# A two-layer MLP on one core: another load schedule, one VectorE semaphore, and a finer split of the last output tile

## Chip, cores, metric

One core of one Trainium2 chip. The metric is the device time of one execution in microseconds (us), as a median of several executions; lower is better. "Span" is the part of an execution that the profile covers; here the time is the span plus about 2.1 us. "Granted clock" is the TensorE clock that the chip allowed, as a share of full speed. An execution counts as fast when it is no more than 1.5% above the fastest of its kernel; all comparisons use fast executions unless the text says otherwise.

## The reference

```python
# B, S, D, F = 1, 2048, 640, 1536, everything bf16
def reference(x, w1, b1, w2, b2):
    h = jnp.einsum("bsd,df->bsf", x, w1) + b1
    r = jnp.where(h > 0, h, 0)
    h = r * r
    return jnp.einsum("bsf,fd->bsd", h, w2) + b2
```

The kernel feeds its first product with x transposed, D on the partitions (`xT`).

## The kernel before

The 2048 tokens are cut into four chunks of 512. PE (the TensorE) works in this order: dummy matmuls, transposes of chunk 0 on PE, first product of chunk 0, first product of chunk 1, second product of chunk 0, first product of chunk 2, second product of chunk 1, and so on. A first-product group is 5 matmuls of 512 columns, a second-product group 12 matmuls of 320 columns. ScalarE applies the relu, VectorE squares, and VectorE also adds b2 and writes the output tile ("eviction").

x arrives in two ways. Chunks 0 and 1 are loaded as they are and transposed on PE with an identity matrix, into PSUM, from where VectorE copies them to `xT`. Chunks 2 and 3 are transposed by the DMA engines. The transposes of chunk 1 stand between groups of chunk 0's first product:

```python
for ft in range(FT):
    G1(ft, 0, CH)
    while tc1 and tc1[0] == ft:            # t_c1_after = (7, 8, 9, 10)
        tc1.pop(0)
        items.append(("T", ...))           # one token tile of chunk 1: 5 PE transposes
...
# sync engine: plain loads first, and only when all have landed the DMA transposes
xn_load(0); xn_load(1)
for i in range(len(w1pieces)): w1_load(i)
for h in range(2, NXH): xn_load(h)         # chunk 1, plain
# ... waits for every load of x, b1, w1, b2, w2 ...
for i, (r0, n) in enumerate(xpieces):      # chunks 2 and 3
    sp.dma_start_transpose(out=xT[:, :, r0:r0 + n], in_=x2[r0:r0 + n, :]).then_inc(sx[i], 16)
for (t, c0, ncols, need) in stores:
    sp.wait_ge(s_o, need)
    sp.dma_start(out=..., in_=o_sb[:, t, c0:c0 + ncols]).then_inc(s_out, 16)
# ... b2 and w2 are loaded by GpSimd once w1 has landed
```

VectorE runs the same item list in order: for `("T", st)` it copies a transposed tile from PSUM, for a first-product group it squares, for a second-product group it evicts. Each kind has its own semaphore (`s_cb`, `s_c`, `s_sq`, `s_o`). The last output tile is two groups of 320 columns, each stored by itself.

## Time and profile before

| | before |
|---|---|
| time, median | 117.18 us (116.68 to 117.58, 4 runs) |
| span of the profiled execution | 114.604 us |
| PE busy | 110.3 us (96%) |
| first matmul of the first product starts | 6.35 us |
| last matmul ends | 112.07 us |

The head of the page of before: span, then busy time of each engine with its share of the span.

```profile
span 114.6 us, 1595 instructions
PE 110.3 (96%) x683; PEld 65.6 (57%) x683; DVE 39.8 (35%) x91; ACT 34.5 (30%) x50; POOL 4.0 (4%) x10
```

PE is the limit. Where PE loses time is told by the chain of waits of before: start, duration, engine and line, number of instructions. L289 are dummies, L310 PE transposes, L237 the copy to `xT`, L342 the first product, L368 the second, L256 the eviction.

```profile
1.12 3.17 PE ps L289 x15
4.29 0.29 PE ps L310 x5
4.61 1.70 DVE xT L237 x4
6.35 8.81 PE ps L342 x40
15.16 0.28 PE ps L310 x5
15.44 1.08 PE ps L342 x5
...
19.27 0.70 ACT r_sb L215
19.97 0.02 issue
19.99 0.42 DVE h2T L244
20.42 0.41 DVE xT L237
20.83 0.05 issue
20.88 13.12 PE ps L342 x60
34.00 13.04 PE ps L368 x96
47.04 12.95 PE ps L342 x60
...
85.98 26.09 PE ps L368 x192
112.07 0.02 issue
112.10 0.49 DVE o_sb L256
```

Read it as a budget. An undisturbed chunk of 60 first-product matmuls takes 12.95 us (216 ns each), 96 second-product matmuls 13.04 us (136 ns each). Between 15.16 and 20.88 us two things stand in the way: PE spends 0.28 us on each of four token tiles of chunk 1, and then the chain leaves PE. Chunk 1 cannot start before the last of its copies, which stands on VectorE behind a square, which waits for a relu. From 6.35 to 34.00 us two chunks of first product take 27.65 us; at 216 ns a matmul the 120 would take 25.9.

Four DMA transposes ran alone in before. The view of stretches (stretch, its length, busy time and count of each engine, PE clock, DMA share, GB/s) shows the DMA engines full at half the rate of plain loads (175 GB/s at a DMA share of 1.00, beside 358 at 1.09; over the neighbouring stretches 175 to 179, beside 327 to 358):

```profile
8.50:10.50 2.00, 2.00 (x11) 0.92 (x10) 0.78 (x2) 1.37 (x2) 0.00 (x0) 1.00 1.09 358
24.50:26.50 2.00, 2.00 (x12) 0.88 (x10) 0.80 (x2) 1.22 (x3) 0.00 (x0) 1.00 1.00 175
```

The last store in the timeline of before is issued 0.03 us after the last eviction ends (112.10 + 0.49 = 112.59):

```profile
112.62 0.33 SPq L202 DMA_DIRECT2D out_dram<-o_sb  x1
```

### The profile page before, as it was taken

Reading aid. Unit: us, or ns where it says so; the run is one execution under the profiler, and the core shown is the slowest. Engines: PE = TensorE matmul, PEld = TensorE weight load, DVE = VectorE, ACT = ScalarE, POOL = GpSimd, SP = SyncE. Lnnn points to the kernel's source line nnn. Section 1 sums busy time; section 2 is a strip of 40 time slices with the busy share of each in tenths; the row PEclk is TensorE's granted clock in tenths of the full one; section 3 lists DMA queues with packets and bytes.
Section 4 is the critical chain, followed back from the end, with each engine's and each line's share of the span. In section 5 each row is a group of like instructions: output and inputs, shape, how many; then the busy total and the mean of one; then the engine's idle time right before and its main releaser. Section 6 shows DMA issues by size and latency. Waiting matters only on the chain.

```text
span 114.6 us, 1595 instructions
## 1 busy us (share of the span) xinstructions
PE 110.3 (96%) x683; PEld 65.6 (57%) x683; DVE 39.8 (35%) x91; ACT 34.5 (30%) x50; POOL 4.0 (4%) x10
## 2 busy tenths in 40 slices
PE   6989999999999999999999999999999999999991
PEld 4834455344447777544447777544447777777770
DVE  1323445444343333243343332243433332333231
ACT  5026564465761000156651000157562000000000
POOL 4000900000000000000000000000000000000000
PEclk9999999999999999999999999999999999999999
DMA  2999499069900111000000111010000110111111
GB/s 62 348 342 371 89 301 350 30 132 166 160 0 6 57 57 57 33 27 0 0 6 0 57 57 54 10 51 6 0 0 0 57 57 31 32 57 57 57 57 57
DMA packets 11414, 9.43 MB, mean 82 GB/s; under 512 B 5744, under 2 KB 10480, under 8 KB 11408
## 3 DMA queue, kind: packets, MB, share of 16 engines
q1 hardware_dynamic: 10896, 7.21, 22.3%
q0 software_dynamic: 512, 2.13, 5.8%
q8 instruction: 5, 0.08, 0.3%
q14 instruction: 1, 0.01, 0.0%
HBM read 5.41 MB, written 2.62 MB: 70 GB/s over the span
## 4 chain that ended last, share of the span: by engine, by line
PE 94%; DVE 3%; ACT 1%; issue 0%
PE ps L368 46%; PE ps L342 45%; PE ps L289 3%; DVE xT L237 2%; PE ps L310 1%; ACT r_sb L215 1%; DVE o_sb L256 0%; DVE h2T L244 0%; DVE scr L225 0%
## 5 line engine op out<-in xcount | busy, mean ns | idle before, releaser
L342 PE MATMUL ps<-xT,w1s 128*128 128x512 bf16 x240 | 53.1, 379 | 0.6 <-DVE xT L237 0.6
L368 PE MATMUL ps<-w2s,h2T 128*128 128x320 bf16 x384 | 52.6, 299 | 0.0
L215 ACT ACTIVATE r_sb<-ps,b1s 128x512 bf16<-128x512 f32 x48 | 33.0, 687 | 51.4 <-PE ps L342 51.4
L368 PEld LDWEIGHTS ps<-w2s,h2T 128*128 128x128 bf16 x384 | 37.6, 98 | 15.1
L342 PEld LDWEIGHTS ps<-xT,w1s 128*128 128x128 bf16 x240 | 23.1, 98 | 28.0 <-DVE xT L237 1.4
L244 DVE TENSOR_TENSOR h2T<-r_sb 128x512 bf16<-128x512 bf16 x48 | 20.4, 426 | 34.0 <-ACT r_sb L215 34.0
L256 DVE TENSOR_TENSOR o_sb<-ps,b2s 128x320 bf16<-128x320 f32 x32 | 15.7, 492 | 34.5 <-PE ps L368 34.5
L237 DVE COPY xT<-ps 128x640 bf16<-128x640 bf16 x8 | 3.6, 484 | 3.4 <-PE ps L310 3.4
L289 PE MATMUL ps<-scr 128*128 128x256 bf16 x18 | 3.7, 381 | 1.1 <-DVE scr L225 1.1
L289 PEld LDWEIGHTS ps<-scr 128*128 128x128 bf16 x18 | 2.3, 137 | 1.9 <-DVE scr L225 1.1
L310 PEld LDWEIGHTS ps<-ident,xn 128*128 128x128 bf16 x40 | 2.7, 98 | 1.0
L310 PE MATMUL ps<-ident,xn 128*128 128x128 bf16 x40 | 3.1, 219 | 0.0
L388 POOL DMA_DIRECT2D w2s<-in_w_dram x3 | 2.3, 763 | 0.0
L208 ACT ACT_TABLE_LOAD x1 | 1.3, 1283 | 0.8 <-PEq L402 0.8
L386 POOL DMA_DIRECT2D b2s<-in_b_dram x1 | 0.6, 615 | 8.9 <-DMA w1s<-in_w_dram 8.9
L379 POOL DMA_DIRECT2D b1row<-in_b_dram x1 | 0.7, 664 | 0.8 <-POOLq L402 0.8
L225 DVE MEMSET scr<- 128x128 f32 x1 | 0.2, 165 | 0.9 <-PEq L402 0.9
L381 POOL TENSOR_SCALAR_AFFINE_SELECT ident<-ones 128x128 bf16<-128x128 bf16 x1 | 0.3, 314 | 0.1
L208 ACT ACTIVATE scr<-scr 128x8 bf16<-128x8 bf16 x1 | 0.2, 208 | 0.0
L294 PE MATMUL ps<-ident,b1row 12*128 12x12 bf16 x1 | 0.2, 176 | 0.0
L226 DVE MEMSET ones<- 128x128 bf16 x1 | 0.2, 165 | 0.0
L232 DVE COPY b1s<-ps 128x12 bf16<-128x12 bf16 x1 | 0.2, 155 | 0.0
(5 smaller groups left out, 0.5 us busy)
## 6 DMA issues: line engine op xcount, KB each, us to landing
out_dram<-o_sb SPq DMA_DIRECT2D x15, 160.0 KB, 1.8
w2s<-in_w_dram POOLq DMA_DIRECT2D x3, 640.0 KB, 7.9
xn<-in_x_dram SPq DMA_DIRECT2D x4, 320.0 KB, 5.1
w1s<-in_w_dram SPq DMA_DIRECT2D x2, 640.0 KB, 6.7
w1s<-in_w_dram SPq DMA_DIRECT2D x2, 320.0 KB, 4.7
b2s<-in_b_dram POOLq DMA_DIRECT2D x1, 160.0 KB, 4.2
out_dram<-o_sb SPq DMA_DIRECT2D x2, 80.0 KB, 1.6
xT<-in_x_dram SPq DMA_TRANSPOSE x4, 4.7
```

Source lines behind the costliest of these rows:

```text
L208: act.activation(out=scr2[:], in_=scr[:, 0:8], func=ACT_FN.Relu)
L215: act.activation(out=r_sb[:, ft, c0:c0 + ncols], in_=ps[:, gi % 4, 0:ncols], func=ACT_FN.Relu, bias=b1s[:, ft:ft + 1], scale=1.0,).then_in ...
L237: v.tensor_copy(out=xT[:, :, st * P:(st + 1) * P], in_=psT(st)[:, 0:KT * P].rearrange("p (k c) -> p k c", k=KT),).then_inc(s_c, 1)
L244: v.tensor_tensor(out=h2T[:, ft, c0:c0 + ncols], in0=r_sb[:, ft, c0:c0 + ncols], in1=r_sb[:, ft, c0:c0 + ncols], op=AluOpType.mult,).then_ ...
L256: v.tensor_tensor(out=o_sb[:, t, c0:c0 + ncols], in0=ps[:, 4 + qi % 4, 0:ncols], in1=b2s[:, c0:c0 + ncols], op=AluOpType.add,).then_inc(s_ ...
L289: pe.matmul(ps[:, bank, 0:256], scr[:, 0:P], scr[:, 0:256], start=True, stop=True)
L310: mm = pe.transpose(out=psT(st)[:, k * P:(k + 1) * P], in_=xn[:, st, k * P:(k + 1) * P], identity=ident[:],)
L342: mm = pe.matmul(ps[:, gi % 4, 0:ncols], w1s[:, k, ft * P:(ft + 1) * P], xT[:, k, c0:c0 + ncols], start=(k == 0), stop=(k == KT - 1),)
L368: mm = pe.matmul(ps[:, 4 + qi % 4, 0:ncols], h2T[:, ft, t * P:(t + 1) * P], w2s[:, ft, c0:c0 + ncols], start=(ft == 0), stop=(ft == FT - 1),)
L379: g.dma_start(out=b1row[:], in_=b1.rearrange("(ft p) -> ft p", p=P)).then_inc(s_b1, 16)
L386: g.dma_start(out=b2s[:], in_=b2.partition_broadcast(P)).then_inc(s_b2, 16)
L388: g.dma_start(out=w2s[:, f0:f0 + n, :], in_=w2v[:, f0:f0 + n, :]).then_inc(sw2[i], 16)
```

## The change

Four edits with these intents: chunk 1 also comes by DMA transpose, queued right behind w1, so PE does not transpose it; b2 and w2 go to the same sync queue and no transfer waits for another any more; all VectorE results count on one semaphore and one-time waits are hoisted into the group before the one that needs them, to save waits at group heads; the last output tile is cut into 320, 192, 64 and 64 columns, so that the last eviction and store are short.

```diff
-    t_c1_after=(7, 8, 9, 10),
+    last_split=(320, 192, 64, 64),
...
-    NXN = 2 * STC
+    NXN = STC
-    xpieces = [(r0, XR) for r0 in range(2 * CH, S, XR)]
+    xpieces = [(r0, XR) for r0 in range(CH, S, XR)]
...
             if t == ST - 1:
+                c0 = 0
+                for n in cfg["last_split"]:
+                    G2(t, c0, n)
+                    c0 += n
...
-        while tc1 and tc1[0] == ft:
-            tc1.pop(0)
-            items.append(("T", STC + (len(cfg["t_c1_after"]) - len(tc1)) - 1))
... sync engine
+            for h in range(NXH):
+                xn_load(h)
             for i in range(len(w1pieces)):
                 w1_load(i)
-            (waits for all loads)
+            xT_load(1)
+            sp.dma_start(out=b2s[:], ...).then_inc(s_b2, 16)
+            for (f0, n) in w2pieces:
+                sp.dma_start(out=w2s[...], in_=w2v[...]).then_inc(s_w2, 16)
+            for c in range(2, NCH):
+                xT_load(c)
... VectorE: every .then_inc(s_cb | s_c | s_sq | s_o, 1) becomes
+            .then_inc(s_dve, 1)            # waiters use the position in VectorE's order
... PE: a one-time wait of the next group goes between matmuls of this one
+                        if k >= 1 and hoist:
+                            hk, he = hoist.pop(0)
+                            once(hk, he)
```

More of the change, by code (lines that the diff above doesn't have):

```diff
@@ L38, in bass_standalone__dense_activation_squared_relu__prompt_kernel @@
     HALF = D // 2
-    NXN = 2 * STC
+    NXN = STC
+    NXH = NXN // 2
     assert D % P == 0 and F % P == 0 and S % CH == 0 and HALF <= 512 and KT * P * 2 <= 2048
-    assert NCH >= 3 and FT <= P
+    assert NCH >= 2 and FT <= P and sum(cfg["last_split"]) == D
     x2 = x.rearrange("b s d -> (b s) d")
     out2 = out.rearrange("b s d -> (b s) d")
-    xnv = x2.rearrange("(st p) d -> p st d", p=P)
     w1v = w1.rearrange("(kt p) f -> p kt f", p=P)
@@ L50, in bass_standalone__dense_activation_squared_relu__prompt_kernel @@
     XR = 256
-    xpieces = [(r0, XR) for r0 in range(2 * CH, S, XR)]
+    xpieces = [(r0, XR) for r0 in range(CH, S, XR)]
     w1pieces = [(0, 2), (2, 2), (4, 4), (8, 4)]
     w2pieces = [(0, 4), (4, 4), (8, 4)]
-    NXH = NXN // 2
     items = []
@@ L69, in G2chunk @@
         for t in range(c * STC, (c + 1) * STC):
-            G2(t, 0, HALF)
-            G2(t, HALF, HALF)
+            if t == ST - 1:
+                c0 = 0
+                for n in cfg["last_split"]:
+                    G2(t, c0, n)
+                    c0 += n
+            else:
+                G2(t, 0, HALF)
+                G2(t, HALF, HALF)
     pad = cfg["pad"]
@@ L82, in bass_standalone__dense_activation_squared_relu__prompt_kernel @@
     items.append(("D", pad[2]))
-    tc1 = list(cfg["t_c1_after"])
     for ft in range(FT):
         G1(ft, 0, CH)
-        while tc1 and tc1[0] == ft:
-            tc1.pop(0)
-            items.append(("T", STC + (len(cfg["t_c1_after"]) - len(tc1)) - 1))
-    assert not tc1
     p1_count_after_chunk[0] = cnt["g1"]
@@ L127, in bass_standalone__dense_activation_squared_relu__prompt_kernel @@
         s_b2 = sem("s_b2")
+        s_w2 = sem("s_w2")
         s_trb = sem("s_trb")
-        s_cb = sem("s_cb")
         s_tr = sem("s_tr")
-        s_c = sem("s_c")
         s_pe1 = sem("s_pe1")
         s_act = sem("s_act")
-        s_sq = sem("s_sq")
         s_pe2 = sem("s_pe2")
-        s_o = sem("s_o")
+        s_dve = sem("s_dve")
         s_out = sem("s_out")
         sxn = [sem(f"s_xn{i}") for i in range(NXH)]
-        sx = [sem(f"s_x{i}") for i in range(len(xpieces))]
+        sxc = [None] + [sem(f"s_xc{c}") for c in range(1, NCH)]
         sw1 = [sem(f"s_w1_{i}") for i in range(len(w1pieces))]
-        sw2 = [sem(f"s_w2_{i}") for i in range(len(w2pieces))]
+        n_xp_chunk = CH // XR
         def piece_of(pieces, idx):
@@ L158, in out_rows @@
             return outv[:, t, :]
+        dve_done = {}
+        n_dve = 0
+        for it in items:
+            if it[0] == "TB":
+                n_dve += 1
+                dve_done[("cb",)] = n_dve
+            elif it[0] == "T":
+                n_dve += 1
+                dve_done[("c", it[1])] = n_dve
+            elif it[0] == "G1":
+                n_dve += 1
+                dve_done[("sq", it[1])] = n_dve
+            elif it[0] == "G2":
+                n_dve += 1
+                dve_done[("ev", it[1])] = n_dve
         stores = []
@@ L165, in bass_standalone__dense_activation_squared_relu__prompt_kernel @@
             if t == ST - 1:
-                stores.append((t, c0, ncols, qi + 1))
+                stores.append((t, c0, ncols, dve_done[("ev", qi)]))
             elif c0 + ncols == D:
-                stores.append((t, 0, D, qi + 1))
+                stores.append((t, 0, D, dve_done[("ev", qi)]))
         @block.sync
@@ L180, in w1_load, with xT_load @@
                 sp.dma_start(out=w1s[:, :, f0 * P:(f0 + n) * P], in_=w1v[:, :, f0 * P:(f0 + n) * P]).then_inc(sw1[i], 16)
-            xn_load(0)
-            xn_load(1)
+            def xT_load(c):
+                for (r0, n) in xpieces:
+                    if r0 // CH == c:
+                        sp.dma_start_transpose(out=xT[:, :, r0:r0 + n], in_=x2[r0:r0 + n, :]).then_inc(sxc[c], 16)
+            for h in range(NXH):
+                xn_load(h)
             for i in range(len(w1pieces)):
                 w1_load(i)
-            for h in range(2, NXH):
-                xn_load(h)
-            for h in range(NXH):
-                sp.wait_ge(sxn[h], 16)
-            sp.wait_ge(s_b1, 16)
-            for i in range(len(w1pieces)):
-                sp.wait_ge(sw1[i], 16)
-            sp.wait_ge(s_b2, 16)
-            for j in range(len(w2pieces)):
-                sp.wait_ge(sw2[j], 16)
-            for i, (r0, n) in enumerate(xpieces):
-                sp.dma_start_transpose(out=xT[:, :, r0:r0 + n], in_=x2[r0:r0 + n, :]).then_inc(sx[i], 16)
-            for i in range(len(xpieces)):
-                sp.wait_ge(sx[i], 16)
+            xT_load(1)
+            sp.dma_start(out=b2s[:], in_=b2.partition_broadcast(P)).then_inc(s_b2, 16)
+            for (f0, n) in w2pieces:
+                sp.dma_start(out=w2s[:, f0:f0 + n, :], in_=w2v[:, f0:f0 + n, :]).then_inc(s_w2, 16)
+            for c in range(2, NCH):
+                xT_load(c)
             for (t, c0, ncols, need) in stores:
-                sp.wait_ge(s_o, need)
+                sp.wait_ge(s_dve, need)
                 sp.dma_start(out=out_rows(t)[:, c0:c0 + ncols], in_=o_sb[:, t, c0:c0 + ncols]).then_inc(s_out, 16)
@@ L208, in _ @@
             act.activation(out=scr2[:], in_=scr[:, 0:8], func=ACT_FN.Relu)
-            act.wait_ge(s_cb, 1)
+            act.wait_ge(s_dve, dve_done[("cb",)])
             for it in items:
@@ L231, in _ @@
                     v.wait_ge(s_trb, 1)
-                    v.tensor_copy(out=b1s[:], in_=b1T_ps).then_inc(s_cb, 1)
+                    v.tensor_copy(out=b1s[:], in_=b1T_ps).then_inc(s_dve, 1)
                 elif it[0] == "T":
@@ L239, in _ @@
                         in_=psT(st)[:, 0:KT * P].rearrange("p (k c) -> p k c", k=KT),
-                    ).then_inc(s_c, 1)
+                    ).then_inc(s_dve, 1)
                 elif it[0] == "G1":
@@ L248, in _ @@
                         op=AluOpType.mult,
-                    ).then_inc(s_sq, 1)
+                    ).then_inc(s_dve, 1)
                 elif it[0] == "G2":
@@ L260, in _ @@
                         op=AluOpType.add,
-                    ).then_inc(s_o, 1)
+                    ).then_inc(s_dve, 1)
         @block.tensor
@@ L265, in _, with wait_dve, once, one_time_waits @@
             pe.wait_ge(s_scr, 1)
-            seen_x = set()
-            seen_xn = set()
-            seen_w1 = set()
-            seen_w2 = set()
-            c_waited = 0
-            n_t = 0
-            n_d = 0
-            first_T = True
-            first_p2 = True
-            cb_waited = False
-            seen_T = set()
-            n_g1 = 0
-            t_bank_users = {}
-            for it in items:
+            state = dict(dve=0, n_t=0, n_d=0, n_g1=0)
+            seen_T = set()
+            seen = set()
+            t_order = [i2[1] for i2 in items if i2[0] == "T"]
+            def wait_dve(v):
+                if v > state["dve"]:
+                    pe.wait_ge(s_dve, v)
+                    state["dve"] = v
+            def once(key, emit):
+                if key not in seen:
+                    emit()
+                    seen.add(key)
+            def one_time_waits(it):
+                res = []
+                if it[0] == "G1":
+                    _, gi, ft, c0, ncols = it
+                    c = c0 // CH
+                    if c >= 1:
+                        res.append((("xc", c), lambda c=c: pe.wait_ge(sxc[c], 16 * n_xp_chunk)))
+                    wi = piece_of(w1pieces, ft)
+                    res.append((("w1", wi), lambda wi=wi: pe.wait_ge(sw1[wi], 16)))
+                elif it[0] == "G2":
+                    res.append((("w2",), lambda: pe.wait_ge(s_w2, 16 * len(w2pieces))))
+                return res
+            for idx, it in enumerate(items):
+                nxt = items[idx + 1] if idx + 1 < len(items) else None
+                hoist = []
+                if nxt is not None and nxt[0] in ("G1", "G2") and it[0] in ("G1", "G2") and state["n_g1"] >= 4:
+                    hoist = [(k, e) for (k, e) in one_time_waits(nxt) if k not in seen]
                 if it[0] == "D":
                     for i in range(it[1]):
-                        if n_t == 0:
-                            bank = 4 + n_d % 4
+                        if state["n_t"] == 0:
+                            bank = 4 + state["n_d"] % 4
                         elif 3 not in seen_T:
@@ L286, in _ @@
                         else:
-                            assert n_g1 == 0
+                            assert state["n_g1"] == 0
                             bank = 2
                         pe.matmul(ps[:, bank, 0:256], scr[:, 0:P], scr[:, 0:256], start=True, stop=True)
-                        n_d += 1
+                        state["n_d"] += 1
                 elif it[0] == "TB":
-                    pe.wait_ge(s_ident, 1)
+                    once(("ident",), lambda: pe.wait_ge(s_ident, 1))
                     pe.wait_ge(s_b1, 16)
@@ L296, in _ @@
                     st = it[1]
-                    if first_T:
-                        pe.wait_ge(s_ident, 1)
-                        first_T = False
+                    once(("ident",), lambda: pe.wait_ge(s_ident, 1))
                     xi = st // 2
-                    if xi not in seen_xn:
-                        pe.wait_ge(sxn[xi], 16)
-                        seen_xn.add(xi)
-                    bank = 4 + st % 4
-                    if bank in t_bank_users:
-                        if t_bank_users[bank] > c_waited:
-                            pe.wait_ge(s_c, t_bank_users[bank])
-                            c_waited = t_bank_users[bank]
+                    once(("xn", xi), lambda: pe.wait_ge(sxn[xi], 16))
                     for k in range(KT):
@@ L314, in _ @@
                         )
-                    n_t += 1
+                    state["n_t"] += 1
                     seen_T.add(st)
                     mm.then_inc(s_tr, 1)
-                    t_bank_users[bank] = n_t
                 elif it[0] == "G1":
                     _, gi, ft, c0, ncols = it
-                    if c0 < 2 * CH:
-                        t_order = [i2[1] for i2 in items if i2[0] == "T"]
-                        need_c = max(t_order.index(st) for st in range(c0 // P, (c0 + ncols - 1) // P + 1)) + 1
-                        if need_c > c_waited:
-                            pe.wait_ge(s_c, need_c)
-                            c_waited = need_c
-                    else:
-                        for xx in range(piece_of(xpieces, c0), piece_of(xpieces, c0 + ncols - 1) + 1):
-                            if xx not in seen_x:
-                                pe.wait_ge(sx[xx], 16)
-                                seen_x.add(xx)
-                    wi = piece_of(w1pieces, ft)
-                    if wi not in seen_w1:
-                        pe.wait_ge(sw1[wi], 16)
-                        seen_w1.add(wi)
-                    if gi % 4 == 3 and not cb_waited:
-                        pe.wait_ge(s_cb, 1)
-                        cb_waited = True
+                    c = c0 // CH
+                    if c == 0:
+                        wait_dve(max(dve_done[("c", st)] for st in range(c0 // P, (c0 + ncols - 1) // P + 1)))
+                    for (k, e) in one_time_waits(it):
+                        once(k, e)
+                    if gi % 4 == 3:
+                        wait_dve(dve_done[("cb",)])
                     if gi >= 4:
@@ L349, in _ @@
                     mm.then_inc(s_pe1, 1)
-                    n_g1 += 1
+                    state["n_g1"] += 1
                 elif it[0] == "G2":
@@ L353, in _ @@
                     c = t // STC
-                    if first_p2:
-                        if n_T > c_waited:
-                            pe.wait_ge(s_c, n_T)
-                            c_waited = n_T
-                        first_p2 = False
-                    if t % STC == 0 and c0 == 0:
-                        pe.wait_ge(s_sq, p1_count_after_chunk[c])
+                    for (k, e) in one_time_waits(it):
+                        once(k, e)
+                    need = dve_done[("c", t_order[-1])]
+                    need = max(need, dve_done[("sq", p1_count_after_chunk[c] - 1)])
                     if qi >= 4:
-                        pe.wait_ge(s_o, qi - 3)
+                        need = max(need, dve_done[("ev", qi - 4)])
+                    wait_dve(need)
                     for ft in range(FT):
-                        wi = piece_of(w2pieces, ft)
-                        if wi not in seen_w2:
-                            pe.wait_ge(sw2[wi], 16)
-                            seen_w2.add(wi)
+                        if ft >= 1 and hoist:
+                            hk, he = hoist.pop(0)
+                            once(hk, he)
                         mm = pe.matmul(
@@ L375, in _ @@
                     mm.then_inc(s_pe2, 1)
+                assert not hoist
         @block.gpsimd
@@ L384, in _ @@
             ).then_inc(s_ident, 1)
-            g.wait_ge(sw1[len(w1pieces) - 1], 16)
-            g.dma_start(out=b2s[:], in_=b2.partition_broadcast(P)).then_inc(s_b2, 16)
-            for i, (f0, n) in enumerate(w2pieces):
-                g.dma_start(out=w2s[:, f0:f0 + n, :], in_=w2v[:, f0:f0 + n, :]).then_inc(sw2[i], 16)
 _INS = ['x', 'w1', 'b1', 'w2', 'b2']
```

## The prediction

> **What bounds the kernel now.** TensorE: the page gives PE 96% of the 114.6 us span at full granted clock, and the chain of waits is 94% PE. From the first real matmul (6.35 us) to the end of the last (112.1) are 105.7 us. By the chain, 60 first-product matmuls of 512 columns take 12.95 us (216 ns each), 96 second-product matmuls of 320 columns 13.04 us (136 ns each); all 240 + 384 need 104.0. So only 1.7 us is other work, and the chain shows it between 15.16 and 20.88 us: four groups of five PE transposes for token chunk 1, 0.28 us each (1.12 us), and a gap of 0.4 us before 20.88, where PE waits for the last transposed copy, which stands on VectorE behind a square that waits for ScalarE.
>
> **What the change does.**
> 1. Chunk 1 comes by DMA transpose: those 20 transposes, four copies (483 ns each) and the gap go, all critical. -1.6 us.
> 2. Loads are reordered. PE needs chunk 1 at 6.35 + 12.96 = 19.3 us. Its transposes are issued behind w1 at about 4.5 and 6.3 us. Before moved 330 to 360 GB/s in the load stretch, so 2.6 MB of x and w1 end near 9.7 us; before's four transposes (1.3 MB) ran at 177 GB/s with the DMA engines full, so 0.65 MB takes 3.7 us: landing at 14 to 15.5 us, 4 us early. w2 then ends near 22 us (needed at 32.3), the rest of x near 30 (needed at 45.3). Before kept transposes apart from other transfers.[...] I expect no stall.
> 3. One VectorE semaphore, hoisted waits: about 0. PE groups follow each other at 216 and 136 ns with no seam to remove.
> 4. Last tile 320+192+64+64 instead of 320+320. Twelve matmuls of 192 take 12 x 82 = 0.99 us. At 64 columns each matmul still loads 128-column weights; the 128-column transposes ran at 56 ns with such loads, so I estimate 56 to 60 ns, 0.7 us a group.[...] Together 2.4 against 1.63 us: +0.75. The last eviction falls from 0.49 to 0.21 us (estimate from 492 ns at 320 and 155 ns at 12 columns): -0.28. The last store shrinks from 80 to 16 KB; landing was 1.8 us at 160 KB and 1.6 at 80, so perhaps -0.1[...]. Net +0.4 us: the split loses.
>
> **Sum.** -1.6 + 0.4 = -1.2 us: 116.0 us, range 115.1 to 116.9. Chances: faster by over 2% 0.06, within 2% 0.90, slower by over 2% 0.04.
>
> **What would show each step.** Right: chunk 1's first matmul at about 19.3 us with no idle PE; its transposes landing before 16 us; the 64-column matmuls 56 to 60 ns apart; last matmul ending near 111.2 us, VectorE near 111.5 instead of 112.59; last store landing 1.5 to 1.6 us after issue. Wrong: idle PE near 19 us (transposes slow in company), near 32 us (w2 late), or vanished seams (step 3 worth something).
>
> **What would make it wrong.** Transposes mixed with loads far slower (beyond 4 us late costs time one for one); 64-column matmuls faster than the weight loads suggest (the split then gains) or far slower; a start-up that moves; an overhead outside the span (2.1 us now) that shrinks[...].

Where a cut is marked, in the prediction and in the expectations below, a passage is left out. -1.6 (step 1) and, in step 4, +0.75, -0.28 and -0.1, together +0.4, make -1.2 us and 116.0 us. The 82 ns at 192 columns, written down without a source, lies on the line through before's 216 ns at 512 columns and 136 at 320; measured later: 82.5 ns (after).

## The result and the profile after

| | before | after |
|---|---|---|
| time, median | 117.29 us (116.68 to 117.58, 16 runs) | 115.72 us (115.25 to 116.0, 10 runs) |
| ratio to before, fast runs | | 0.9867 [0.9845, 0.9889] |
| span of the profiled execution | 114.604 us | 113.897 us |
| start of the first product | 6.35 us | 7.24 us |
| start of the first product to the end of the span | 108.25 us | 106.66 us |
| of this: to the first second-product matmul | 27.65 us | 26.07 us |
| of this: from the last matmul's end to the span's end | 2.53 us | 2.46 us |

Ratios are the mean time of one kernel's fast runs over the mean of the other's in the same rounds, so they are not quite the ratio of the medians. The kernel gained 1.57 us, 1.3%.

The head of the page of after:

```profile
span 113.9 us, 1586 instructions
PE 110.3 (97%) x687; PEld 66.2 (58%) x687; DVE 38.8 (34%) x89; ACT 34.5 (30%) x50; POOL 1.2 (1%) x6
```

The chain of waits of after; L320 are dummies, L332 PE transposes, L355 the first product, L378 the second, L267 the eviction:

```profile
1.13 3.38 PE ps L320 x15
4.51 2.13 PE ps L332 x20
...
7.24 26.07 PE ps L355 x120
33.31 13.04 PE ps L378 x96
...
85.29 26.15 PE ps L378 x216
111.44 0.02 issue
111.46 0.23 DVE o_sb L267
```

Three readings. First, chunks 0 and 1 are now one line of 120 matmuls in 26.07 us, 1.58 us less than the same stretch of before; after it, only the last line differs. Second, the last chunk pair has 216 matmuls in place of 192 (24 more, by the finer split), and takes only 0.06 us more. Third, the start moved the wrong way: the 20 PE transposes of chunk 0 took 2.13 us, 106 ns each, where before's of chunk 1 took 56 (0.28/5). The clock changes kept in the packed traces go with it: full clock is on record from 6.67 us in after, when these transposes were over, and from 3.94 us in before, ahead of its own transposes of chunk 0, which start 56 ns apart. The dummies tell the same: 213 ns apart ahead of that record in both traces, 109 ns behind it. (The PE clock column of the stretches shows 1.00 even before its first record, so at the start the spacing has to be read.) The start of the first product is thus a matter of the execution: the two profiles compared were one with an early start (6.35 us; at 116.68 us the fastest of before's runs) and one with a late start (7.24 us; at 116.00 the slowest of after's). Compared raw, they show 0.7 us of gain; the medians show 1.57. From here on profiles are compared from the start of the first product.

The transposes of chunk 1 in the timeline of the sync queue of after, issue start and duration:

```profile
4.59 5.07 SPq L199 DMA_TRANSPOSE xT<-in_x_dram  x1
9.70 2.22 SPq L199 DMA_TRANSPOSE xT<-in_x_dram  x1
```

The view of the DMA gives 8.4 and 4.4 us from issue to landing, so they landed at 13.0 and 14.1 us. Chunk 1 was wanted at about 20.2 us (7.24 plus 60 matmuls of 216 ns). The rest of x had landed by 30.5 us: the DMA moved nothing between 30.5 and 32.5.

The end of the sync queue's timeline in after, two answers for neighbouring stretches (the second merges the last two stores):

```profile
111.53 0.43 SPq L213 DMA_DIRECT2D out_dram<-o_sb  x1
111.53 0.91 SPq L213 DMA_DIRECT2D out_dram<-o_sb  x2
```

The two stores of 64 columns begin at 111.53 and, since each takes 0.43 us to issue, at about 112.01 (111.53 + 0.91 - 0.43). The last eviction was over at 111.69. So the last store stands 0.32 us behind its neighbour on the queue; in before that wait was 0.03.

### The profile page after: what moved, and what is told of

Same layout as the page of the kernel before. It is cut to its first block, busy times and chain, and to the rows that moved or that the text cites. A ratio compares the mean times of both kernels' runs of the same rounds, so it can differ in the third digit from the quotient of the medians.

```text
span 113.9 us, 1586 instructions
## 1 busy us (share of the span) xinstructions
PE 110.3 (97%) x687; PEld 66.2 (58%) x687; DVE 38.8 (34%) x89; ACT 34.5 (30%) x50; POOL 1.2 (1%) x6
## 4 chain that ended last, share of the span: by engine, by line
PE 97%; DVE 0%; issue 0%
PE ps L378 46%; PE ps L355 46%; PE ps L320 3%; PE ps L332 2%; DVE o_sb L267 0%; DVE scr L236 0%; PE ps L325 0%
## 5 line engine op out<-in xcount | busy, mean ns | idle before, releaser
L378 PE MATMUL ps<-w2s,h2T 128*128 128x320 bf16 (+2 forms) x408 | 52.7, 291 | 0.0
L355 PE MATMUL ps<-xT,w1s 128*128 128x512 bf16 x240 | 52.3, 379 | 0.0
L378 PEld LDWEIGHTS ps<-w2s,h2T 128*128 128x128 bf16 x408 | 38.2, 98 | 14.7
L355 PEld LDWEIGHTS ps<-xT,w1s 128*128 128x128 bf16 x240 | 23.4, 98 | 28.1 <-DVE xT L248 0.3
L267 DVE TENSOR_TENSOR o_sb<-ps,b2s 128x320 bf16<-128x320 f32 (+2 forms) x34 | 16.0, 472 | 33.9 <-PE ps L378 33.8
L320 PE MATMUL ps<-scr 128*128 128x256 bf16 x18 | 3.9, 395 | 1.1 <-DVE scr L236 1.1
L320 PEld LDWEIGHTS ps<-scr 128*128 128x128 bf16 x18 | 2.3, 137 | 2.0 <-DVE scr L236 1.1
L248 DVE COPY xT<-ps 128x640 bf16<-128x640 bf16 x4 | 2.0, 492 | 4.0 <-PE ps L332 3.9
L332 PE MATMUL ps<-ident,xn 128*128 128x128 bf16 x20 | 2.3, 314 | 0.0
L332 PEld LDWEIGHTS ps<-ident,xn 128*128 128x128 bf16 x20 | 2.2, 151 | 0.1
```

What stands on the lines that cost most here:

```text
L248: v.tensor_copy(out=xT[:, :, st * P:(st + 1) * P], in_=psT(st)[:, 0:KT * P].rearrange("p (k c) -> p k c", k=KT),).then_inc(s_dve, 1)
L267: v.tensor_tensor(out=o_sb[:, t, c0:c0 + ncols], in0=ps[:, 4 + qi % 4, 0:ncols], in1=b2s[:, c0:c0 + ncols], op=AluOpType.add,).then_inc(s_ ...
L320: pe.matmul(ps[:, bank, 0:256], scr[:, 0:P], scr[:, 0:256], start=True, stop=True)
L332: mm = pe.transpose(out=psT(st)[:, k * P:(k + 1) * P], in_=xn[:, st, k * P:(k + 1) * P], identity=ident[:],)
L355: mm = pe.matmul(ps[:, gi % 4, 0:ncols], w1s[:, k, ft * P:(ft + 1) * P], xT[:, k, c0:c0 + ncols], start=(k == 0), stop=(k == KT - 1),)
L378: mm = pe.matmul(ps[:, 4 + qi % 4, 0:ncols], h2T[:, ft, t * P:(t + 1) * P], w2s[:, ft, c0:c0 + ncols], start=(ft == 0), stop=(ft == FT - 1),)
```

## The experiments

Theory A, formed from the two traces: the whole gain is the 1.58 us of the stretch of chunks 0 and 1 (PE transposes gone, and the wait for their last copy); the split of the last tile nets zero; semaphore and hoisting are worth nothing. Rivals: the recorded step 4 (the split costs 0.4 us); the split gains; the semaphore part has a share. Each run is correct against the reference. In the table at the end all of them stand side by side.

### e1_tail_whole: after without the split

```diff
-    last_split=(320, 192, 64, 64),
+    last_split=(320, 320),
```

> The kernel after, with the last tile as 320+320 again. Theory A (the split nets about zero: PE pays 0.06 us for the extra matmuls, the last eviction is 0.26 us shorter, and the last store waits about 0.2 us behind the other stores): within 0.15 us of the kernel after, 115.6 to 115.9 us, ratio to before 0.986 to 0.988; last eviction 0.49 us, end of the last matmul to the end of the span about 2.52 us against 2.46. Rival R (the recorded step 4: the split costs 0.4 us): 115.3 us, ratio 0.983. Rival S (the split gains its 0.3 us of shorter eviction and landing): 116.0 us, ratio 0.989.

Measured: 115.98 us (4 runs), ratio 0.9888 [0.9867, 0.9910], against 0.9867 [0.9845, 0.9889] of after in other rounds: the time alone lies where the rival S of the expectation had it (116.0 us, 0.989) and just outside the range of theory A, but the intervals overlap and the times cannot tell the two apart. The profile can: from the start of the first product to the end of the span 106.66 us, the same as after to a hundredth. The recorded -0.4 would have read 106.3, a gain of 0.3 by the split 107.0. The split nets zero.

### e2_before_split: before with the split alone

```diff
-            G2(t, 0, HALF)
-            G2(t, HALF, HALF)
+            (320, 192, 64, 64 for the last tile, as in the change)
```

> The kernel before with the 320+192+64+64 split alone. Theory A: same as before within 0.15 us, ratio 0.9990 to 1.0013; the 24 matmuls of 64 columns start 29 ns apart. Rival R: +0.4 us, ratio 1.0034, and 56 to 60 ns apart. Rival S: -0.3 us, ratio 0.9974.

Measured: 117.27 us, ratio 0.9997 [0.9969, 1.0024]; start of the first product to the end of the span 108.28 us, before 108.25. The last 216 matmuls take 26.15 us. Of these, 180 have 320 columns (24.45 us at before's 135.85 ns), 12 have 192 (0.99 us), which leaves 0.71 us for 24 of 64 columns, at most 29.5 ns each. The starts in the packed trace say the same directly: in after as in e2 the matmuls of 192 columns start 82.5 ns apart and those of 64 columns 29 ns. (e6 below, with 12 of 192 and 12 of 128 columns, fits: 26.12 us.) Same answer from the other side: zero.

### e3_pe_transposes: after with chunk 1 transposed on PE

```diff
-    NXN = STC
+    NXN = 2 * STC
...
         G1(ft, 0, CH)
+        if 7 <= ft <= 10:
+            items.append(("T", STC + ft - 7))
... (chunk 1 leaves the list of DMA transposes; its first product waits for the copies)
-            xT_load(1)
+            for h in range(2, NXH):
+                xn_load(h)
```

> The kernel after with chunk 1 transposed on PE again, as before had it; merged semaphore, hoisted waits and split stay. Theory A: all 1.58 us come back, as 1.1 us of PE transposes and 0.4 us of waiting for the last copy: ratio to before 0.998 to 1.002; from the first matmul of the first product to that of the first second-product group 27.6 us as in before (26.1 in after). Rival T (merged semaphore and hoisted waits earn a part of it): ratio 0.990 to 0.996.

Measured: 117.44 us, ratio 1.0008 [0.9987, 1.0028]. The stretch of chunks 0 and 1 is 27.65 us again, the whole from the first product's start 108.24. In the chain of waits of e3 (L358 the first product, L251 the copy to `xT`, L381 the second product) the detour over VectorE is back:

```profile
7.08 2.33 PE ps L358 x10
...
21.15 0.41 DVE xT L251
...
34.73 13.04 PE ps L381 x96
```

Merged semaphore, hoisted waits, new queue for w2 and the split are all in this kernel, and together they are worth nothing that can be measured here. All of the gain hangs on who transposes chunk 1.

### e4_no_hoist: after without hoisting

```diff
-                    hoist = [(k, e) for (k, e) in one_time_waits(nxt) if k not in seen]
+                    hoist = []
```

> The kernel after without hoisting: one-time waits stand again at the head of their own group. Theory A: the waits are long met[...]: same as after, ratio to before 0.986 to 0.988, and the 120 matmuls of the first two chunks take 26.07 us again. Rival T: ratio above 0.990, with steps of 50 ns or more between groups at the first matmul of chunks 1, 2, 3.

Measured: 115.71 us, ratio 0.9865 [0.9842, 0.9888]; the stretch of the first two chunks 26.07 us, the whole 106.66. Hoisting earns nothing here: the data are there long before (in after chunk 1 had landed at 14.1 us and was wanted at about 20.2). (The chain of e4 has pieces of 0.05 us called "issue"; they stand where the trace lacks a matmul record, 233 of 240 being kept, and e8, which hoists, has them at the same places.)

### e5_narrow32: the spacing of narrow matmuls by itself

```diff
-    last_split=(320, 192, 64, 64),
+    last_split=(320,) + (32,) * 10,
```

> The kernel after with the last tile as 320 + ten groups of 32 columns, to measure the spacing of narrow matmuls by itself (not to be fast). In after the 24 of 64 columns came 29 ns apart. Theory P[...] the 120 narrow matmuls take 1.9 us. Rival F[...]: 3.0 to 3.5 us. Rival R (the recorded 56 ns floor): 6.7 us. The stores of ten groups at 0.33 to 0.43 us each on the sync queue should outlast the matmuls, so the end is set by them.

(Theory P carries the line through 216 ns at 512 columns and 136 at 320, that is 0.417 ns a column and 2.5 ns, on to 32 columns: 16 ns each. The range of rival F comes to 25 to 29 ns each; 29 is the spacing of 64 columns in after, 25 had no run behind it before this one.)

Measured (one look): 120.17 us. The chain of waits of e5 gives the last 300 matmuls:

```profile
85.15 27.46 PE ps L378 x300
```

Less 24.45 us for the 180 of 320 columns, the 120 of 32 columns take 3.01 us, 25 ns each. Theory P (16 ns) falls, rival F (25 to 29 ns) stands; what sets the 25 ns, this run does not tell. The granted clock was full until the last matmul (the lower mean of this run, 0.988, comes from after it). So matmuls that each load new weights come 216 ns apart at 512 columns, 136 at 320, 56 at 128 (PE transposes), 29 at 64 and 25 at 32: on that line down to 64, and 9 ns above it at 32. And as expected the stores outlast the matmuls:

```profile
111.96 4.66 SPq L213 DMA_DIRECT2D out_dram<-o_sb  x7
```

The sync queue is still issuing stores until 116.6 us, four microseconds after PE is done. They go out one after another: six of these seven issues took 0.43 us each, one took 1.80 (why is not known).

### e6_tail_128: one store less at the end

```diff
-    last_split=(320, 192, 64, 64),
+    last_split=(320, 192, 128),
```

> The kernel after with 320+192+128 in place of 320+192+64+64: one store less at the end. Theory B (the last store of after waits about 0.3 us behind the store before it on the sync queue): the last store is issued about 0.34 us after the end of the last matmul instead of 0.57, the end of the last matmul to the end of the span is 2.20 to 2.30 us instead of 2.46, and the time is 0.2 us below after_again of the same call. Rival (the 128-column eviction costs what the free queue gains, or landing of small stores is what sets the end): 2.4 to 2.5 us, no change of time.

Measured: 115.56 us (114.8 to 115.66), ratio 0.9847 [0.9816, 0.9877], beside 115.88 us for after. The end of the chain of waits of e6:

```profile
85.19 26.12 PE ps L378 x204
111.31 0.02 issue
111.33 0.29 DVE o_sb L267
```

and its last store in the timeline:

```profile
111.65 0.33 SPq L213 DMA_DIRECT2D out_dram<-o_sb  x1
```

The last eviction is 0.06 us longer than with 64 columns, but the store goes out 0.03 us after it (111.33 + 0.29 = 111.62), 0.34 us after the last matmul, where after took 0.57. From the last matmul to the span's end are 2.17 us, 2.46 in after; a little more than expected was saved. From the first product's start 106.35 us, 0.31 less than after. The queue of the stores was what ate the shorter eviction. (The narrow stores also took longer to issue: 0.43 us at 64 columns, 0.33 at 128 and more.) This is the fastest version; over after it gains 0.3 us by the trace, and the intervals of the two ratios (after: [0.9851, 0.9907]) overlap.

### e7_late_transposes: chunk 1 behind w2

```diff
-            xT_load(1)
             sp.dma_start(out=b2s[:], ...)
             (w2 loads)
-            for c in range(2, NCH):
+            for c in range(1, NCH):
                 xT_load(c)
```

> The kernel after with the two transposes of chunk 1 behind b2 and w2 instead of ahead of them. Theory A (arrival counts only against the deadline): they land about 6 us later than the 13.0 and 14.1 us of after, at 19 to 22 us; PE then stalls for the landing less the 20.2 us at which chunk 1 is wanted, 0 to 2 us, and the time is after plus that stall, one for one. Rival (order of loads is free, nothing waits on it): no stall and no change. Rival (transposes side by side with w2 hurt each other): stall above 2 us.

Measured: 118.40 us median, but with two levels: three executions at full granted clock took 118.24 to 118.40, two at a mean of 0.986 took 119.92 and 121.01. The profile is of one of the latter. Its PE timeline:

```profile
21.57 1.04 PE L354 MATMUL ps<-xT,w1s 128*128 128x512 bf16 x4 [2.35 <-DMA xT<-in_x_dram]
22.80 5.38 PE L354 MATMUL ps<-xT,w1s 128*128 128x512 bf16 x17 [0.19 <-issue]
```

Chunk 1 landed at 21.5 us, within the expected range, and PE stood 2.35 us. The expectation had the stall run from 20.2 us, at most 2 us. It began a microsecond earlier, at 19.2 us: this execution started its first product 0.28 us before after's, and the hoisted wait stands after the first matmul of chunk 0's last group, so that the other four (0.86 us) wait too. The theory was right about "one for one" and wrong about where the deadline is. Then comes something that was not expected, in the stretches of the same execution (the last three columns are PE clock, DMA share, GB/s):

```profile
19.00:21.50 2.50, 0.22 (x2) 0.00 (x0) 0.54 (x2) 0.69 (x1) 0.00 (x0) 1.00 0.69 151
21.50:23.00 1.50, 1.24 (x5) 0.65 (x7) 0.00 (x0) 0.35 (x1) 0.00 (x0) 0.84 0.92 185
23.00:26.00 3.00, 3.00 (x8) 1.03 (x7) 0.85 (x2) 1.02 (x2) 0.00 (x0) 0.51 1.02 202
26.00:28.00 2.00, 2.00 (x10) 0.88 (x9) 0.42 (x1) 1.11 (x2) 0.00 (x0) 1.00 0.78 125
```

Right after the stall the granted clock falls to 0.51 for some 3 us and returns to 1.00. The clock changes in the packed trace put the half clock from 22.52 to 25.93 us, 3.41 us. In the chain of waits of this execution 49 matmuls from 22.80 us on took 12.29 us, where 49 take 10.74 in e10. In this execution the stall was followed by a second loss, 1.55 us. That the idle time caused the drop is argued from the order of events, not tried by itself. The stretches between two recorded clock changes are 17.07 us (full, 5.45 to 22.52) and 3.41 us (half) in e7, 112.64 us in before and 109.23 in after (both full): 5, 1, 33 and 32 times 3.413 us. Why, and why the drop came here, was not shown; after the 2.02 us of e10 below none came. Among the executions at full clock the delay is 2.4 us over after (medians 118.29 and 115.88), about the size of the stall; their own traces were not kept.

### e8_after_again: a second profile of after

> The kernel after unchanged, for a second profile and for the comparison with e6. From the start of the first product's first matmul to the end of the last matmul 104.2 us as in the first profile of after; the start of that matmul itself moves between executions from 6.3 to 7.3 us whatever the kernel (6.35 in before, 7.24 in after, 6.82 in e2, which starts as before does), so span and time move by as much.

Measured: 115.88 us, ratio 0.9879 [0.9851, 0.9907]. First product's start at 7.18 us, 106.66 us from there, 104.20 us to the last matmul's end: the same as in the first profile. The starts of all profiles lie between 6.35 and 7.24 us. What they follow is said at the end of the account below. They are too few to say whether the change moves the start on average; if it does, it is by little, since from the first product on after is 1.59 us shorter and the medians differ by 1.57 and 1.41 us.

### e9_earlier_transposes: before with its PE transposes two groups earlier

```diff
-    t_c1_after=(7, 8, 9, 10),
+    t_c1_after=(5, 6, 7, 8),
```

> The kernel before with the four PE transposes of chunk 1 placed two groups earlier, after groups 5 to 8 in place of 7 to 10; still on PE. Theory A splits the 1.58 us into 1.1 us of PE time of the transposes and about 0.45 us of waiting for the last copy. Placed earlier the copy is long done, so only the wait goes: from the first group's start to the first second-product group 27.2 us instead of 27.65, ratio to before 0.9955 to 0.9975. Rival: the wait is part of the price of the transposes (their copies always end late) and stays: ratio 0.999 to 1.001.

Measured: 117.04 us, ratio 0.9976 [0.9954, 0.9997], 0.0001 outside the range expected. The trace is clearer: the stretch of chunks 0 and 1 is 27.18 us (27.65 in before), the whole 107.79 (108.25). In the chain of e9 the four transposes remain and the detour over ScalarE and VectorE is gone:

```profile
17.84 0.28 PE ps L310 x5
18.12 0.05 issue
18.18 10.74 PE ps L342 x49
```

So 0.47 us of the 1.58 was a wait that a better place for the transposes would have avoided without any DMA transpose; the other 1.1 us was PE time.

### e10_late_no_hoist: e7 without hoisting

```diff
 (e7)
-                    hoist = [(k, e) for (k, e) in one_time_waits(nxt) if k not in seen]
+                    hoist = []
```

> The kernel e7 (chunk 1 transposed late, landing at 21.5 us) without hoisting. Theory H (the hoisted wait stands after the first matmul of the group before, so a late arrival also holds up that group's other four matmuls): the stall starts at 20.0 instead of 19.1 us and is 0.86 us shorter, so fast executions at full granted clock take about 117.5 us in place of 118.3. Rival (where the wait stands is of no account): 118.3 us again.

Measured: 117.41 us (117.37 to 117.75), all four executions at full granted clock, 0.9 us below e7's full-clock executions. PE stood 2.02 us:

```profile
21.84 3.40 PE L354 MATMUL ps<-xT,w1s 128*128 128x512 bf16 x15 [2.02 <-DMA xT<-in_x_dram]
```

Hoisting a wait brings its deadline forward. It earned nothing where data was early (e4), and it cost 0.9 us where data was late.

### Side by side

Profile columns: start of the first product (A), first product of chunks 0 and 1 (B), last matmul's end to the span's end (C), A's point to the span's end (D), all us.

| kernel | median us (fast runs) | ratio to before | A | B | C | D |
|---|---|---|---|---|---|---|
| before | 117.29 (16) | 1 | 6.35 | 27.65 | 2.53 | 108.25 |
| after | 115.72 (10) | 0.9867 | 7.24 | 26.07 | 2.46 | 106.66 |
| e8, after again | 115.88 (6) | 0.9879 | 7.18 | 26.07 | 2.46 | 106.66 |
| e1, no split | 115.98 (4) | 0.9888 | 7.16 | 26.08 | 2.51 | 106.66 |
| e4, no hoist | 115.71 (4) | 0.9865 | 7.06 | 26.07 | 2.46 | 106.66 |
| e6, 320+192+128 | 115.56 (6) | 0.9847 | 7.13 | 26.08 | 2.17 | 106.35 |
| e2, before + split | 117.27 (6) | 0.9997 | 6.82 | 27.65 | 2.50 | 108.28 |
| e3, PE transposes back | 117.44 (6) | 1.0008 | 7.08 | 27.65 | 2.46 | 108.24 |
| e9, earlier transposes | 117.04 (6) | 0.9976 | 7.13 | 27.18 | 2.55 | 107.79 |
| e10, late, no hoist | 117.41 (4) | 1.0023 | 6.69 | 28.05 | 2.47 | 108.65 |

The kernels fall into groups by B, and B accounts for nearly all of D. e5 is left out as a measurement only, e7 because its profile ran partly at half clock (A 6.96, span 117.846).

## Why the prediction was right, and where it was not

Predicted 116.0 us, measured 115.72: inside the range, and the gain somewhat larger than predicted. The sum of steps was -1.6 + 0.4; the runs say -1.58 and 0.0.

- **Step 1, the PE transposes and the gap (-1.6 us): right, shown.** 27.65 to 26.07 us in the trace; e3 gives all of it back; e9 splits it into 0.47 us of wait and 1.1 us of transposes.
- **Step 2, chunk 1 in time, no stall: right, shown.** Landing at 13.0 and 14.1 us (predicted 14 to 15.5). The way there was not as predicted: the second transpose was not issued at 6.3 but at 9.70 us, since the first held the sync queue for 5.07 us; both landed in time all the same. e7 shows that the place ahead of w2 is needed: behind w2 it stalls PE. The results were correct with the transposes next to ordinary DMAs, and the transposes landed no later than the bytes ahead of them and before's rates had predicted.
- **Step 3, semaphore and hoisting (about 0): right, shown** by e3 and e4.
- **Step 4, the split (+0.4 us, "the split loses"): wrong; it nets 0.0 (e1, e2).** The step that failed is the term of the 64-column matmuls. It put 56 to 60 ns on each, because "each matmul still loads 128-column weights; the 128-column transposes ran at 56 ns with such loads". But 56 ns at 128 columns lies on the line through before's own 216 ns at 512 columns and 136 at 320, which gives 56 at 128, and 29 at 64. So those transposes said only that a weight load needs no more than 56 ns. Measured at 64 columns: 29 ns, and the PE term is +0.06 us where +0.75 was predicted. Below 64 columns the line did not hold: e5 measures 25 ns at 32 columns, where it gives 16. The eviction term was right (0.49 to 0.23 us, predicted 0.21). The last store's term was mis-sized the other way: -0.1 was predicted. Landing did get shorter (80 KB took 1.6 us, 16 KB 1.5), but 0.3 us was lost in waiting behind the other small stores, which the prediction did not consider. (It had named faster 64-column matmuls as a way to be wrong, and expected the split to gain then; because of this queue it did not.) e6 takes a store away and gets that time back.
- **The check that matched for the wrong reason.** The prediction named 111.2 us for the last matmul's end and 111.5 for VectorE's; the profile has 111.44 and 111.69. That looks like agreement, but the start was 0.89 us later than in before's profile and the matmuls of the split 0.69 us shorter than thought. Only the stretches from the first product's start tell the steps apart.

What the early or late start goes with in each execution, the packed traces show: the moment at which the granted clock becomes full. It is on record for all profiles but e2's, from 3.94 us (before, start at 6.35) over 4.65 (e10, 6.69) and 5.45 (e7, 6.96) to 6.67 (after, 7.24), and the starts come in the same order; ahead of that moment the dummies and transposes run at half speed (213 and 106 ns apart in after), behind it at full (109 and 56 ns in before). The one exception is e9, full from 5.71 us but starting at 7.13, where the first product waited for the first piece of w1, landed at 7.00. What stays open is why the clock becomes full when it does in a given execution. Whether e6's 0.3 us shows in the times beyond doubt stays open too: the trace has it, the intervals overlap.

## What to carry to other kernels

On a kernel bound by PE, look in the chain of waits for stretches where PE does what another unit could do, and for the places where the chain leaves PE; here these two were the whole gain, and a DMA transpose that landed early cost PE nothing to speak of (120 matmuls in 26.07 us, beside 25.9 at 216 ns each). A spacing set by one limit says of a limit hidden below it only that it is no larger (here 56 ns at 128 columns of the weight load): find a case that separates the two before you build on it. When the tail is cut finer, count the stores as well as the columns, since each store takes its turn at the issuing queue (0.33 to 0.43 us here), and compare profiles from a common event inside the span when the start moves between executions.
